# Two early transfers, the early weight conversions and one batch's halves, each issued sooner in a fused attention and mixer kernel

## The chip, the cores and the metric

The kernel runs on one core of one Trainium2 chip. The metric is device time in microseconds (us), from the first to the last instruction of the program with what the runtime adds around it, median of three runs.

## What is computed

Three layers follow each other; the arrays are float64, four batches, twelve heads, sequence 448, head size 64, so 768 features.

```python
# 1 attention with a sigmoid
scores = q @ k.T / 8 - log(448)
attn = (1 / (1 + exp(-scores))) @ v          # -> x [4, 448, 768]
# 2 mixer
h = x.T @ U @ V                              # along the sequence, U 448x32, V 32x448
u = x + h.T
x = u + relu(u @ w_ch1) @ w_ch2              # 768 -> 3072 -> 768
# 3 second mixer
theta = x @ w_theta
y = w_tok_r @ (x * cos(theta)) + w_tok_i @ (x * sin(theta))
u = x + y
out = u + relu(u @ w_ch)
```

## The kernel before

**Numbers in two halves.** Every matrix operand is split into a rounded high half and the rest (names ending in `h` and `l`), and a product is the sum of high by high, high by low and low by high. ScalarE makes the high half (`hi_act`, line 109), VectorE (`lo_dve`, line 121) or GpSimd (`lo_pool`, line 112) the low half by a subtraction.

**Attention.** Two heads form a pair; there are 24 pairs (`NP`), six to a batch, and the loop `for p in range(NP)` takes one after the other. For pair p it computes the scores in two parts, `QK(p, 0)` and `QK(p, 1)`, of two tiles `sc` each (line 386; 12 products a part). PSUM has two `sc` buffers, and ScalarE's sigmoid (line 390, tile `A`) frees them. `AV` (line 399) multiplies the `A` of pair p-1 by its values `v`, two of four steps after each part of the scores, into the one PSUM buffer `av`, which ScalarE empties into `X`. `XN(p-2)` (line 412) transposes a finished pair. While pair p is computed, VectorE prepares pair p+1: transposes into `kT` and `qT` (lines 364, 350), the high half `qh` (354) and the low halves `ql` and `kl` (121).

**The first mixer inside attention.** When a batch b is complete, `U1` (line 423, in pair 6b+8) and `U2` (line 448, tile `h`, in pairs 6b+9 to 6b+11) compute x.T @ U @ V for it and add it to `X`. `U2` needs `vcat`, the converted V.

**Conversions.** Weights come as float64 words. A `Conv` job turns one block into float32 halves in five steps: `size` (ScalarE, line 146; it also issues the load of the job after next), `shift` (VectorE, 150 and 153), `sign` (159, 162), `low` (167) and `fin`, which splits on ScalarE and GpSimd (183 and 184 for a weight, 112 and 115 for V). The nine early jobs are, in order, w1_0_0, U, V0, V1, w2_0_0, w1_0_1, w2_0_1, w1_1_0 and w2_1_0: 45 steps, handed out by `early_step()` one at a time. Before, two are handed out in each pair from pair 2 on, one between `K_hi(p + 1)` and `K_lo(p + 1)` and one at the pair's end, and what is left comes after the loop. Step 15 of 45, the `fin` of V0, so falls into pair 9 just ahead of `U2`.

**Queues.** The order on each engine is the order in which the program is written. Transfers are issued by SyncE's queue (SP) and a few at the start by ScalarE's. A pair takes four transfers of k, four of q (32x14x32) and two of v (112x4x64). Each transfer takes one of eight completion semaphores in turn (named DMAHW0 to DMAHW7 in the order below), and waits at its issue until the earlier transfer with the same semaphore has landed. Loads of k and q are issued four pairs ahead, of v three.

**The handover.** After the last pair, `split_u(0, ...)` makes the halves `uh` and `ul` of batch 0 (six columns d), the last pair's `AV` follows, then `split_u(1, ...)`, whose low halves go to GpSimd and VectorE in turn, `XN(22)`, and `ch1(0, 0)` (lines 620 to 622, tile `g`): two tiles of 18 products, which need the six `uh` and `ul` one after another.

Of the kernel before, what the change touches and what calls it, by code (L numbers as in the profile page):

```python
# [12 lines left out]
F32R = mybir.dt.float32r  # L13
# [11 lines left out]
def tile_kernel(  # L25
# [15 lines left out]
    nc = tc.nc  # L41
    B, H, S, D = q.shape
# [3 lines left out]
    P = 128  # L46
    CP = 112
    NC = S // CP
    NK = DM // P
# [40 lines left out]
    X = cpool.tile([P, NK, NT], F32, name="X")  # L90
# [9 lines left out]
    def pool(name, side="left", space=None):  # L100
        st = ExitStack()
        kw = dict(name=name, bufs=1, side=side, reuse_waits="tile")
        if space is not None:
            kw["space"] = space
        return st.enter_context(tc.tile_pool(**kw)), st


    def hi_act(o, i):
        nc.scalar.activation(o, i, AF.Copy)  # L109
# [10 lines left out]
    def lo_dve(o, i, h):  # L120
        nc.vector.tensor_sub(o, i, f(h))  # L121
# [187 lines left out]
    ap2, ap2_st = pool("ap2")  # L309
# [10 lines left out]
    def load_squares(eng, t, src):  # L320

        for h in range(2):
            for n in range(2):
                a = 2 * h + n
                eng.dma_start(
                    out=t[a * SQ:(a + 1) * SQ],
                    in_=src[h, :, n * SQ:(n + 1) * SQ].rearrange("(k i) j -> i k j", i=SQ),
                )

    def load_qk(p):  # L330
        b, hp = divmod(p, NH)
        h0 = 2 * hp
        kt = ap2.tile([P, NS, SQ], F32, tag="k", name=f"k_{p}", bufs=4)
        qt = ap2.tile([P, NS, SQ], F32, tag="q", name=f"q_{p}", bufs=4)
        load_squares(nc.sync, kt, k[b, h0:h0 + 2])
        load_squares(nc.scalar if p == 0 else nc.sync, qt, q[b, h0:h0 + 2])
        q_t[p], k_t[p] = qt, kt

    def load_v(p, eng=nc.sync):
        b, hp = divmod(p, NH)  # L340
        vt = ap1.tile([CP, 2, NC, D], F32, tag="v", name=f"v_{p}", bufs=4)
        for h in range(2):
            eng.dma_start(out=vt[:, h], in_=v[b, 2 * hp + h].rearrange("(c p) d -> p c d", p=CP))
        v_t[p] = vt

    def TQ(p):
        t = q_t.pop(p).rearrange("p k j -> p (k j)")
        x = ap2.tile([P, S], F32, tag="qT", name=f"qT_{p}", bufs=2)
        for n, s, m in runs(p // NH, 0, S):
            nc.vector.transpose(out=x[:, n:n + m], in_=t[:, s:s + m])  # L350
        h_ = ap2.tile([P, S], F32R, tag="qh", name=f"qh_{p}", bufs=2)
        l_ = ap2.tile([P, S], F32R, tag="ql", name=f"ql_{p}", bufs=2)
        if p:
            nc.vector.tensor_copy(h_, x)
        else:
            hi_act(h_, x)
        qq_t[p] = (h_, l_)
        return lambda: lo_dve(l_, x, h_)
# [3 lines left out]
    def TK(p):  # L362
        x = ap2.tile([P, S], F32, tag="kT", name=f"kT_{p}", bufs=2)
        nc.vector.transpose(out=x, in_=k_t.pop(p).rearrange("p k j -> p (k j)"))
        kT_t[p] = x

    def K_hi(p):
        h_ = ap2.tile([P, S], F32R, tag="kh", name=f"kh_{p}", bufs=2)
        l_ = ap2.tile([P, S], F32R, tag="kl", name=f"kl_{p}", bufs=2)
        kk_t[p] = (h_, l_)  # L370
        hi_act(h_, kT_t[p])

    def K_lo(p):
        h_, l_ = kk_t[p]
        lo_dve(l_, kT_t.pop(p), h_)

    def QK(p, half):


        (kh, kl), (qh, ql) = kk_t[p], qq_t[p]  # L380
        for c in (2 * half, 2 * half + 1):
            ps = ps_b.tile([P, 2, 512], F32, tag="sc", name=f"sc_{p}_{c}", bufs=2)
            for n, (a, b) in enumerate(((kh, qh), (kh, ql), (kl, qh))):
                for h in range(2):
                    sl = slice(h * D, (h + 1) * D)
                    nc.tensor.matmul(  # L386
                        ps[:CP, h, :S], a[sl, c * CP:(c + 1) * CP], b[sl], start=n == 0, stop=n == 2
                    )
            a = ap1.tile([CP, 2, S], F32, tag="A", name=f"A_{p}_{c}", bufs=6)
            nc.scalar.activation(a, ps[:CP, :, :S], AF.Sigmoid, bias=bias_s[:CP], scale=SCALE)  # L390
            A_t[p, c] = a

    def AV(p, c):
        b, hp = divmod(p, NH)
        if c == 0:
            av_t[p] = ps_a.tile([P, 512], F32, tag="av", name=f"av_{p}")
        ps = av_t[p]
        for h in range(2):
            nc.tensor.matmul(  # L399
                ps[h * D:(h + 1) * D, :S], v_t[p][:, h, c, :], A_t[p, c][:, h, :],  # L400
                start=c == 0, stop=c == NC - 1,
            )
        if c == NC - 1:
            hi_act(X[:, hp, b * S:(b + 1) * S], ps[:, :S])

    def XN(p):
        b, hp = divmod(p, NH)
        if hp == 0:
            xn_t[b] = ap.tile([CP, NC, DM], F32, tag="xn", name=f"xn_{b}")
        ps = ps_a.tile([P, 512], F32, tag="qx", name=f"xt_{p}")  # L410
        for c in range(NC):
            nc.tensor.transpose(ps[:CP, c * P:(c + 1) * P], X[:, hp, b * S + c * CP:b * S + (c + 1) * CP], ident)
        nc.vector.tensor_copy(
            xn_t[b][:, :, hp * P:(hp + 1) * P], ps[:CP].rearrange("p (c n) -> p c n", c=NC)
        )
# [20 lines left out]
    def u1_lo():  # L436

        while u1_t:
            ps, o = u1_t.pop()
            for g in range(3):  # L440
                x = ps[g * R:(g + 1) * R, :2 * P]
                sl = slice(2 * g * P, 2 * (g + 1) * P)
                for m in range(2):
                    lo_dve(o[(2 + m) * R:(3 + m) * R, sl], x, o[:R, sl])

    def U2(b, d, ps, vc, n=1):
        for m in range(n):
            nc.tensor.matmul(
                ps[:, m, :S], pc_t[b][:, (d + m) * P:(d + m + 1) * P], vc, start=True, stop=True
            )  # L450
        x = X[:, d:d + n, b * S:(b + 1) * S]
        nc.vector.tensor_add(x, ps[:, :n, :S], x)
# [75 lines left out]
    load_qk(0)  # L528
    nc.scalar.activation(warm, bias_s, AF.Sigmoid)
    load_v(0, nc.scalar)  # L530
    load_qk(1)
    load_qk(2)
    seq[0].load()
# [5 lines left out]
    def early_step():  # L539
        if esteps:  # L540
            esteps.pop(0).step()


    def warm_up(n):
        ps = ps_b.tile([P, 2, 512], F32, tag="sc", name=f"warm_{n}", bufs=2)
        for m in range(n):
            nc.tensor.transpose(ps[:, m % 2, :P], ident, ident)

    warm_up(36)
    TK(0)  # L550
    K_hi(0)
    lo_q = TQ(0)
    K_lo(0)
    lo_q()
    load_v(1, nc.scalar)
    for p in range(NP):
        nx = p + 1 < NP
        QK(p, 0)
        if nx:
            TK(p + 1)  # L560
            TQ(p + 1)()
        if p:
            AV(p - 1, 0)
            AV(p - 1, 1)
        if nx:
            K_hi(p + 1)
        if p > 1:
            early_step()
        if nx:
            K_lo(p + 1)  # L570
        b, r = divmod(p - 3 - NH, NH)
        if b >= 0 and r < NK // 2:
            U2(b, 2 * r, ps_a.tile([P, 2, 512], F32, tag="ux", name=f"h_{b}_{r}"), vcat[:, b % 2, :], 2)
        QK(p, 1)
        if p > 1:
            XN(p - 2)
        b, r = divmod(p - 2 - NH, NH)
        if b >= 0 and r == 0:
            U1(b, ap)
        if p:  # L580
            AV(p - 1, 2)
            AV(p - 1, 3)
        u1_lo()
        if p + 4 < NP:
            load_qk(p + 4)
        if 2 < p + 3 < NP:
            load_v(p + 3)
        if p == 0:
            seq[1].load()
        if p > 1:  # L590
            early_step()
    while esteps:
        early_step()
    ap2_st.close()
    ps_b_st.close()


    u01, u01_st = pool("u01", "right")
    ps_g, ps_g_st = pool("ps_g", "right", PSUM)
    uh_t, ul_t, g_t = {}, {}, {}  # L600

    def split_u(b, p, d0, d1, *los):
        if d0 == 0:
            uh_t[b] = p.tile([P, NK, S], F32R, name=f"uh{b}")
            ul_t[b] = p.tile([P, NK, S], F32R, name=f"ul{b}")
        for d in range(d0, d1):
            x = X[:, d, b * S:(b + 1) * S]
            hi_act(uh_t[b][:, d], x)
            los[d % len(los)](ul_t[b][:, d], x, uh_t[b][:, d])

    def ch1(i, b, js=range(FB)):
        if js[0] == 0:
# [34 lines left out]
            after(e2)  # L647


    split_u(0, u01, 0, NK, lo_dve)  # L650
    for c in range(NC):
        AV(NP - 1, c)
    ap1_st.close()
    uv, uv_st = pool("uv", "right")
    vlast = uv.tile([P, S], F32R, name="vlast")
    split_u(1, u01, 0, NK, lo_pool, lo_dve)
    XN(NP - 2)
    ch1(0, 0)
# [291 lines left out]
```

## Time and profile before

| | us |
|---|---|
| median of 3 runs | 1213.49 (1213.0 to 1218.13) |
| profiled execution, whole time | 1212.33 |
| its span, first to last instruction | 1210.5 |
| TensorE (PE) busy | 1178.9 (97%) |
| VectorE (DVE) busy | 784.4 (65%) |
| ScalarE (ACT) busy | 377.9 (31%) |
| GpSimd (POOL) busy | 298.9 (25%) |

The attention stage covers about the first 205 us of the span, the two big products of the first mixer the next 800, the second mixer the rest. PE is busy nearly everywhere; the 32 us in which it is not are spread over few places. A row of the timeline gives start, duration, engine, source line, operation, tile written from tiles read, and in brackets how long the engine had been idle and what released it. "x8" means eight instructions merged into one row. PEld is PE's weight load, SPq and ACTq are the issues of transfers.

### The profile page before, as it was taken

How to read it: one execution, taken by the hardware profiler on the slowest of the kernel's cores; microseconds unless marked ns; L12 is line 12 of the kernel's file. 1: busy time of each engine (PE TensorE's matmuls, PEld its weight loads, DVE VectorE, ACT ScalarE, POOL GpSimd, SP SyncE). 2: the span in 40 equal slices, each digit the busy share in tenths (PEclk: the TensorE clock that was granted, in tenths of full speed). 3: DMA queues.
4: the chain of work that ended last, by engine and by line, in shares of the span. 5: the costliest groups of instructions: out<-in, count | busy, mean ns of one | idle time of the engine just before them, and what ended most of it. 6: DMA issues, size and time to landing. Idle time of an engine off the chain costs nothing.

```text
span 1210.5 us, 15584 instructions
## 1 busy us (share of the span) xinstructions
PE 1178.9 (97%) x6220; PEld 1017.9 (84%) x6220; DVE 784.4 (65%) x955; ACT 377.9 (31%) x498; POOL 298.9 (25%) x170
## 2 busy tenths in 40 slices
PE   5979998999999999999999999999999999999998
PEld 3434444899999999999999999999999999999997
DVE  3656778456886678677867787969465733733443
ACT  3756786222221212122212221322123531531110
POOL 0111124232232314132322233434201512320000
PEclk7999999999999999999999999999999999999999
DMA  7664761001223122222322232333452000030344
GB/s 138 128 130 96 148 132 53 2 27 53 94 68 109 53 94 76 101 73 74 109 68 79 71 117 98 111 105 105 144 198 106 1 1 1 1 157 1 47 66 71
DMA packets 190808, 99.88 MB, mean 83 GB/s; under 512 B 158736, under 2 KB 182672, under 8 KB 190608
## 3 DMA queue, kind: packets, MB, share of 16 engines
q1 hardware_dynamic: 164752, 95.45, 28.2%
q10 hardware_dynamic: 25984, 3.44, 2.0%
q8 instruction: 49, 0.80, 0.3%
q14 instruction: 23, 0.19, 0.1%
HBM read 80.71 MB, written 18.15 MB: 82 GB/s over the span
## 4 chain that ended last, share of the span: by engine, by line
PE 92%; DVE 2%; SPq 2%; DMA 1%; ACT 1%; issue 1%; POOL 0%; ACTq 0%; DVEq 0%; POOLq 0%
PE g L621 10%; PE g L622 10%; PE g L620 10%; PE y L642 9%; PE y L644 9%; PE y L643 9%; PE av L399 5%; PE sc L386 5%; PE y L831 3%; PE y L832 3%; PE y L833 3%; PE th L754 2%; PE th L758 2%; PE th L755 2%; PE wc L912 2%; PE wc L913 2%
## 5 line engine op out<-in xcount | busy, mean ns | idle before, releaser
L621 PE MATMUL g<-ul,w 128*128 128x448 f32 x576 | 211.0, 366 | 2.6 <-DVE ul L121 2.6
L642 PE MATMUL y<-gh,w 128*128 128x448 f32 x576 | 211.3, 367 | 0.7 <-DVE X L646 0.7
L620 PE MATMUL g<-uh,w 128*128 128x448 f32 x576 | 210.8, 366 | 0.0
L644 PE MATMUL y<-gh,w 128*128 128x448 f32 x576 | 210.5, 365 | 0.0
L622 PE MATMUL g<-uh,w 128*128 128x448 f32 x576 | 210.5, 365 | 0.0
L643 PE MATMUL y<-gl,w 128*128 128x448 f32 x576 | 210.4, 365 | 0.0
L646 DVE TENSOR_TENSOR X<-y,X 128x896 f32<-128x896 f32 x144 | 156.3, 1087 | 79.1 <-PE y L644 77.6
L183 POOL TENSOR_TENSOR ca_w<-ca_w,w 128x768 f32<-128x768 f32 x48 | 90.3, 1881 | 470.0 <-ACT w L109 470.0
L627 ACT ACTIVATE gh<-g 128x896 fp32r<-128x896 f32 x48 | 44.1, 919 | 335.1 <-PE g L622 335.1
L621 PEld LDWEIGHTS g<-ul,w 128*128 128x128 f32 x576 | 108.2, 188 | 12.7 <-DVE ul L121 4.1
L628 DVE SCALAR_TENSOR_TENSOR gl<-g,gh 128x896 fp32r<-128x896 f32 x48 | 52.3, 1091 | 101.6 <-ACT gh L627 101.6
L642 PEld LDWEIGHTS y<-gh,w 128*128 128x128 f32 x576 | 108.2, 188 | 9.8 <-issue 1.1
L620 PEld LDWEIGHTS g<-uh,w 128*128 128x128 f32 x576 | 108.2, 188 | 9.1 <-issue 0.4
L644 PEld LDWEIGHTS y<-gh,w 128*128 128x128 f32 x576 | 108.2, 188 | 8.7
L622 PEld LDWEIGHTS g<-uh,w 128*128 128x128 f32 x576 | 108.2, 188 | 8.6
L643 PEld LDWEIGHTS y<-gl,w 128*128 128x128 f32 x576 | 108.2, 188 | 8.5
L390 ACT ACTIVATE A<-sc,bias_s 112x896 f32<-112x896 f32 x96 | 91.6, 1004 | 36.6 <-PE sc L386 24.3
L184 POOL TENSOR_TENSOR w<-ca_w,ws_w 128x768 fp32r<-128x768 f32 x48 | 96.1, 2003 | 3.8
L399 PE MATMUL av<-A,v 112*64 112x448 f32 x384 | 83.4, 557 | 0.6 <-ACT X L109 0.6
L112 POOL TENSOR_TENSOR zl<-t,zh 128x768 fp32r<-128x768 f32 x23 | 42.7, 1881 | 114.2 <-ACT zh L109 114.2
L146 ACT ACTIVATE ca_w<-ws_w 128x768 f32<-128x768 f32 x48 | 43.5, 906 | 61.0 <-POOL w L184 55.8
L831 PE MATMUL y<-tok,zh 128*128 128x448 f32 x168 | 61.7, 367 | 0.0
(145 smaller groups left out, 1867.8 us busy)
## 6 DMA issues: line engine op xcount, KB each, us to landing
ws_w<-in_moe_w_ch_dram SPq DMA_DIRECT2D x48, 768.0 KB, 4.5
k<-in_k_dram SPq DMA_DIRECT2D x96, 56.0 KB, 2.7
q<-in_q_dram SPq DMA_DIRECT2D x92, 56.0 KB, 2.4
v<-in_v_dram SPq DMA_DIRECT2D x44, 112.0 KB, 2.8
ws_th<-in_moe_w_theta_dram SPq DMA_DIRECT2D x6, 768.0 KB, 4.5
th_d<-sp_th SPq DMA_DIRECT2D x6, 768.0 KB, 6.3
ws_wc<-in_moe_w_ch_dram SPq DMA_DIRECT2D x6, 768.0 KB, 4.6
wc_d<-sp_wc SPq DMA_DIRECT2D x6, 768.0 KB, 7.0
```

The costliest lines, as they stand in the source:

```text
L183: eng.tensor_sub(a, a, f(o[:, 0]))
L184: eng.tensor_add(o[:, 1], a, e)
L390: nc.scalar.activation(a, ps[:CP, :, :S], AF.Sigmoid, bias=bias_s[:CP], scale=SCALE)
L399: nc.tensor.matmul(ps[h * D:(h + 1) * D, :S], v_t[p][:, h, c, :], A_t[p, c][:, h, :], start=c == 0, stop=c == NC - 1,)
L620: nc.tensor.matmul(o, wh[:, sl], uh_t[b][:, kk, :], start=kk == 0, stop=False)
L621: nc.tensor.matmul(o, wh[:, sl], ul_t[b][:, kk, :], start=False, stop=False)
L622: nc.tensor.matmul(o, wl[:, sl], uh_t[b][:, kk, :], start=False, stop=kk == NK - 1)
L642: nc.tensor.matmul(o, wh[:, sl], gh[:, j, :], start=j == 0, stop=False)
L643: nc.tensor.matmul(o, wh[:, sl], gl[:, j, :], start=False, stop=False)
L644: nc.tensor.matmul(o, wl[:, sl], gh[:, j, :], start=False, stop=j == FB - 1)
L646: nc.vector.tensor_add(x, ps[:, :, :S], x)
L831: nc.tensor.matmul(o, zh[:, sl], tok_h[:, i, :], start=n == 0, stop=False)
```

## The change

Three edits, and a function that moves with the third.

1. `load_v(1, nc.scalar)`, the values of pair 1, is written ahead of `load_qk(1)` instead of after the first pair's conversions.
2. `early_step()` is handed out from pair 1 on instead of pair 2, and a third time in pairs 4 and 6. Step 15, the `fin` of V0, falls into pair 7, and the last of the 45 into pair 22; none is left after the loop.
3. In the last pair the first three columns of `split_u(0, ...)` are written between `QK(23, 1)` and `XN(21)`, the other three at the loop's end. The memory of `ap2` (k, q and their halves) is given back there for it. `split_u` itself is unchanged and only stands earlier.

```diff
     load_qk(0)
     nc.scalar.activation(warm, bias_s, AF.Sigmoid)
     load_v(0, nc.scalar)
+    load_v(1, nc.scalar)
     load_qk(1)
     load_qk(2)
     seq[0].load()
...
     K_lo(0)
     lo_q()
-    load_v(1, nc.scalar)
     for p in range(NP):
...
             K_hi(p + 1)
-        if p > 1:
+        if p:
             early_step()
         if nx:
             K_lo(p + 1)
...
         QK(p, 1)
+        if not nx:
+            ap2_st.close()
+            u01, u01_st = pool("u01", "right")
+            split_u(0, u01, 0, 3, lo_dve)
         if p > 1:
             XN(p - 2)
...
         u1_lo()
+        if p in (4, 6):
+            early_step()
         if p + 4 < NP:
             load_qk(p + 4)
         if 2 < p + 3 < NP:
             load_v(p + 3)
         if p == 0:
             seq[1].load()
-        if p > 1:
+        if p:
             early_step()
+    split_u(0, u01, 3, NK, lo_dve)
     while esteps:
         early_step()
-    ap2_st.close()
     ps_b_st.close()
...
-    u01, u01_st = pool("u01", "right")
     ps_g, ps_g_st = pool("ps_g", "right", PSUM)
...
-    split_u(0, u01, 0, NK, lo_dve)
     for c in range(NC):
         AV(NP - 1, c)
```

ScalarE's order at the start and in pair 1 (`v_198` before and `v_114` now are the values of pair 1; `A_0` to `A_3` the sigmoids of a pair's four score tiles; `ca_w_0_0` the first step of job w1_0_0):

```order
 L343 DMA v_111<-in_v_dram 112x4x64 [waits DMAHW3_49]
-L109 ACTIVATE kh_188<-kT_186 128x448 [waits DVE_49]
-L109 ACTIVATE qh_193<-qT_191 128x448 [waits DVE_49]
-L343 DMA v_198<-in_v_dram 112x4x64 [waits DMAHW4_49]
-L343 DMA v_198<-in_v_dram 112x4x64 [waits DMAHW6_49]
+L343 DMA v_114<-in_v_dram 112x4x64 [waits DMAHW5_49]
+L343 DMA v_114<-in_v_dram 112x4x64 [waits DMAHW6_49]
+L109 ACTIVATE kh_191<-kT_189 128x448 [waits DVE_49]
+L109 ACTIVATE qh_196<-qT_194 128x448 [waits DVE_49]
 L390 ACTIVATE A_0_208<-sc_0_201,bias_s 112x896 [waits PE_49]
 L390 ACTIVATE A_1_217<-sc_1_210,bias_s 112x896 [waits PE_49]
...
 L109 ACTIVATE kh_303<-kT_290 128x448 [waits DVE_49,Activation_49]
...
+L146 ACTIVATE ca_w_0_0_311<-ws_w_0_0_137 128x768 [waits DMAHW4_49]
+L390 ACTIVATE A_2_321<-sc_2_314,bias_s 112x896 [waits PE_49,Activation_49]
```

The two issues move ahead of the first pair's high halves, and their semaphores were last used by transfers of pair 0 instead of pair 3; in pair 1 the first step of w1_0_0 now stands between two sigmoids.

SP's order after U's nine transfers, before (`k_330`, `q_331`, `v_340`: k and q of pair 5, values of pair 4; `ws_V_377`: V0):

```order
L278 DMA ws_U<-in_moe_U_dram 112x64 [waits DMAHW1_49]
L325 DMA k_330<-in_k_dram 32x14x32 [waits DMAHW2_49,DVE_49]
...
L325 DMA q_331<-in_q_dram 32x14x32 [waits DMAHW6_49,DVE_49]
...
L343 DMA v_340<-in_v_dram 112x4x64 [waits DMAHW2_49,PE_49]
L343 DMA v_340<-in_v_dram 112x4x64 [waits DMAHW3_49]
L289 DMA ws_V_377<-in_moe_V_dram 32x896 [waits DMAHW4_49]
```

and now (`ws_V_306`: V0; `k_337`, `q_338`: pair 5):

```order
L278 DMA ws_U<-in_moe_U_dram 112x64 [waits DMAHW1_49]
L289 DMA ws_V_306<-in_moe_V_dram 32x896 [waits DMAHW2_49]
L289 DMA ws_V_306<-in_moe_V_dram 32x896 [waits DMAHW3_49]
L289 DMA ws_V_306<-in_moe_V_dram 32x896 [waits DMAHW4_49]
L289 DMA ws_V_306<-in_moe_V_dram 32x896 [waits DMAHW5_49]
L325 DMA k_337<-in_k_dram 32x14x32 [waits DMAHW6_49,DVE_49]
```

V0's four transfers moved from behind pair 5's k and q to ahead of them.

VectorE's order around the last step of V0 ahead of its `fin`, before (`pc_924`: the result of `U1` for batch 0, pair 8; `kT_974`: pair 10):

```order
L121 TENSOR_TENSOR pc_924<-p_0_911,pc_924 32x256 x5
L167 SCALAR_TENSOR_TENSOR ws_V_377<-ws_V_377 128x448 [waits DVE_49]
L364 STREAM_TRANSPOSE kT_974<-k_750 128x448 [waits DMAHW2_49,DMAHW3_49,DMAHW1_49,DMAHW0_49]
```

and now (`kT_791`: pair 8):

```order
L159 SCALAR_TENSOR_TENSOR ca_V_688<-ws_V_306,ca_V_688 128x448 [waits DVE_49]
L162 TENSOR_SCALAR ws_V_306<-ca_V_688 128x448 [waits DVE_49]
L167 SCALAR_TENSOR_TENSOR ws_V_306<-ws_V_306 128x448 [waits DVE_49]
L364 STREAM_TRANSPOSE kT_791<-k_593 128x448 [waits DMAHW6_49,DMAHW7_49,DMAHW5_49,DMAHW4_49]
```

V0 is ready for its `fin` two pairs sooner, and no longer behind batch 0's `pc`.

## Rows read from the trace of the kernel before

**Rows 1.** Waits of PE over the span: total us, times, longest us.

```profile
PE sc L386 <- ACT A L390: 11.0, 1, 11.0
PE h L448 <- POOL vcat L115: 8.1, 1, 8.1
PE g L621 <- DVE ul L121: 2.6, 4, 0.7
```

**Rows 2.** Timeline of the first 34 us, ScalarE and PE.

```profile
4.39 0.86 ACTq L343 DMA_DIRECT2D v<-in_v_dram  x2
...
18.32 1.14 ACTq L343 DMA_DIRECT2D v<-in_v_dram  x2
...
19.51 1.91 ACT L390 ACTIVATE A<-sc,bias_s 112x896 f32<-112x896 f32 x2 [11.91 <-DMA k<-in_k_dram]
...
20.57 0.72 PE L386 MATMUL sc<-qh,kh 64*112 64x448 f32 x2 [10.97 <-ACT A L390]
...
25.24 1.73 PE L399 MATMUL av<-A,v 112*64 112x448 f32 x8
...
31.37 1.72 PE L399 MATMUL av<-A,v 112*64 112x448 f32 x8
...
33.19 0.90 ACT L146 ACTIVATE ca_w<-ws_w 128x768 f32<-128x768 f32 x1
```

**Rows 3.** Timeline: SP's issues of w1_0_0, of U, of pair 5's q, of V0.

```profile
12.41 0.48 SPq L201 DMA_DIRECT2D ws_w<-in_moe_w_ch_dram  x1
...
25.01 5.42 SPq L278 DMA_DIRECT2D ws_U<-in_moe_U_dram  x9
...
32.56 1.99 SPq L325 DMA_DIRECT2D q<-in_q_dram  x4
...
35.65 1.88 SPq L289 DMA_DIRECT2D ws_V<-in_moe_V_dram  x4
```

**Rows 4.** Issue to landing: first w1_0_0's one transfer, then pair 5's four of q.

```profile
DMA to landing us min/median/max: 5.1/5.1/5.1
...
DMA to landing us min/median/max: 2.2/2.2/2.5
```

**Rows 5.** Timeline: pair 1's q on VectorE, and PE's AV in pair 5.

```profile
10.21 0.65 DVE L350 STREAM_TRANSPOSE qT<-q 128x448 f32<-128x448 f32 x1 [0.64 <-DMA q<-in_q_dram]
...
11.32 0.62 DVE L121 TENSOR_TENSOR ql<-qT,qh 128x448 fp32r<-128x448 f32 x1
...
51.49 1.73 PE L399 MATMUL av<-A,v 112*64 112x448 f32 x8
```

**Rows 6.** Timeline: first scores of pairs 9, 10, 21 and 22 on PE.

```profile
78.77 0.46 PE L386 MATMUL sc<-qh,kh 64*112 64x448 f32 x2
...
97.09 0.46 PE L386 MATMUL sc<-qh,kh 64*112 64x448 f32 x2
...
178.07 0.46 PE L386 MATMUL sc<-qh,kh 64*112 64x448 f32 x2
...
185.76 0.46 PE L386 MATMUL sc<-qh,kh 64*112 64x448 f32 x2
```

**Rows 7.** Busy us (and instructions) of PE, PEld, DVE, ACT, POOL; PEclk; DMA share; GB/s.

```profile
90.00:97.00 7.00, 7.00 (x26) 3.57 (x26) 3.36 (x7) 2.01 (x2) 0.00 (x0) 0.54 0.01 2
```

**Rows 8.** Handover, 201 to 217 us: timeline, and all ul (ns min/median/max).

```profile
202.23 2.90 ACT L109 ACTIVATE uh<-X 128x448 fp32r<-128x448 f32 x6
202.41 1.84 POOL L183 TENSOR_TENSOR ca_w<-ca_w,w 128x768 f32<-128x768 f32 x1 [11.37 <-ACT w L109]
...
205.21 0.45 PE L620 MATMUL g<-uh,w 128*128 128x448 f32 x1
...
212.59 0.37 PE L620 MATMUL g<-uh,w 128*128 128x448 f32 x1
...
216.25 0.60 PE L412 MATMUL xt<-ident,X 128*112 128x128 f32 x4
...
L121 DVE TENSOR_TENSOR ul<-X,uh x9: 609/1564/2283, 202.8 to 212.9; 128x448 fp32r<-128x448 f32 x9
```

More of the change, by code (lines that the diff above doesn't have):

```diff
@@ L547, in warm_up, with split_u @@
             nc.tensor.transpose(ps[:, m % 2, :P], ident, ident)
+    uh_t, ul_t, g_t = {}, {}, {}
+    def split_u(b, p, d0, d1, *los):
+        if d0 == 0:
+            uh_t[b] = p.tile([P, NK, S], F32R, name=f"uh{b}")
+            ul_t[b] = p.tile([P, NK, S], F32R, name=f"ul{b}")
+        for d in range(d0, d1):
+            x = X[:, d, b * S:(b + 1) * S]
+            hi_act(uh_t[b][:, d], x)
+            los[d % len(los)](ul_t[b][:, d], x, uh_t[b][:, d])
     warm_up(36)
@@ L589, in tile_kernel @@
             seq[1].load()
-        if p > 1:
+        if p:
             early_step()
+    split_u(0, u01, 3, NK, lo_dve)
     while esteps:
         early_step()
-    ap2_st.close()
     ps_b_st.close()
-    u01, u01_st = pool("u01", "right")
     ps_g, ps_g_st = pool("ps_g", "right", PSUM)
[L600 to L609, printed above, removed]
     def ch1(i, b, js=range(FB)):
```

## The prediction

> **What bounds the kernel now.** I read first who PE waits for: three waits hold most of its idle time, 11.0 us at the scores, 8.1 at `h`, 2.6 at `g` [rows 1]. All three lie in attention and at its end, and each has one of the three edits beside it. Elsewhere PE works back to back, so a place is worth what its stall holds, and only until the next late thing.
>
> *The start.* ScalarE stands still for 11.91 us before the first sigmoids, put down to a transfer of k [rows 2]. In its queue the issues of pair 1's values stand just ahead, at 18.32 us: they waited for semaphores that pair 3's k held. PE's scores stop for want of a buffer (9.60 to 20.57), and the first `AV` comes at 25.24 [rows 2].
>
> *Pair 9.* `U2` waits for `vcat`, which GpSimd finishes only then. From pair 9's first scores to pair 10's it takes 97.09 - 78.77 = 18.32 us; the same work in pair 21, with no such wait, takes 185.76 - 178.07 = 7.69 [rows 6]. Behind the wait PE also runs at a mean granted clock of 0.54, so mostly at the lower level, 1.2 GHz, after 8.1 us without work [rows 1, 7].
>
> *The handover.* The first tile of `ch1(0, 0)` takes 212.59 - 205.21 = 7.38 us, the second, of the same 18 products, 216.25 - 212.59 = 3.66. The difference, 3.72, is waiting for `ul`, of which one takes 0.61 us at best, 1.56 in the median and 2.28 at worst while GpSimd works on the left-over conversion step and then on its own low halves [rows 8].
>
> **The change, part by part.**
>
> *Values of pair 1 sooner.* Their second issue now needs a semaphore of pair 0's q, landed by the time the first `qT` runs; the two issues cost 0.86 us on ScalarE at 4.39 for pair 0 [rows 2] and the next thing there waits for `kT` anyway, so I take 0.2, between 0 and 0.9. Score tile 0 is then turned by the sigmoid as soon as it is done, some 0.6 before 9.60, so at about 9.0. Before, `AV` followed the first sigmoid after 25.24 - 19.51 = 5.73 us [rows 2], part of it at the lower clock; I take 5.3 (4.8 to 5.7), which puts `AV` at 14.3 plus or minus 0.5, or **10.9 sooner**. That is the most the edit can give. Two things come late next.
>
> *Step 1 of w1_0_0 in pair 1.* It now stands ahead of two sigmoids and waits for its weights. SP issues those at 12.41 and they land 5.1 later [rows 3, 4]. SP's queue itself slips a little, because pair 1's q and pair 2's k now wait for semaphores of the two value loads; I take 0.5 (0 to 1.0, the length of a pair of value issues). So they land at 18.0, the step takes 0.90 [rows 2], and the sigmoids behind it start at 18.9 instead of about 17. The second `AV`, before at 31.37 and wanted at 20.5, comes at about 21.4: 18.9, two sigmoids (1.91 [rows 2]) and the eviction of `av`, for which I take the length of one `uh`, 0.5 [rows 8]. That is 1.0 lost, **9.9 left**.
>
> *Pair 5's q.* SP issues without a pause in this stretch, and what it does does not come sooner because PE does. U's nine transfers still end at 30.4, now 30.9 with the slip. V0's four (1.88) stand ahead of pair 5 [rows 3]. Pair 5's q was issued from 32.56 to 34.55, so now at 32.56 + 0.5 + 2.0 = 35.05 to 37.05; its last transfer is issued at about 36.6 and lands 2.4 later at 39.0 [rows 3, 4]. From a landing to the end of `ql` pair 1 shows 11.32 + 0.62 - 10.21 = 1.73 [rows 5]; then comes U's `shift`, which has a third of a weight's columns (0.6), and `kl` (0.62): 41.95. The `kl` products begin a third into the part, so `AV` follows 0.9 later at 42.85. Before it was at 51.49 [rows 5]: **8.65 sooner**, and that takes the place of the 9.9. The bounds: 9.9 if q comes in time, 7.0 if SP slips by 1.0 and issues a little slower still.
>
> *After pair 5* a pair takes (51.49 - 31.37) / 3 = 6.71 us on PE [rows 2, 5] and 5.1 on SP (1.99 each for k and q, 1 for v), so SP gains 1.6 a pair, less what V1 (eight issues, 3.8) and w2_0_0 take. Adding these up, q of pair 8 and of pair 10 arrive between 0.1 and 1 us ahead of need. I charge nothing, at worst 2.
>
> *V0 two pairs sooner.* Its `fin` moves from pair 9 to pair 7; GpSimd's four operations need some 5 us there and have two pairs, 13.4. `U2` then waits for `pc` alone, as in pair 21. So 18.32 becomes 7.69 plus 0.3 for the `kl` of the next pair, which VectorE's fuller queue delays: **10.3 sooner** (9 to 10.6). It contains the 8.1 of waiting and 2.5 to 2.9 of the lower clock. Every issue it moves (V1, w2_0_0) was counted above on SP.
>
> *Halves of batch 0.* Three `uh` (3 x 0.48 = 1.45) now stand on ScalarE ahead of the eviction that the last `AV` waits for. ScalarE was idle for 0.9 just there, so the last `AV` starts 0.56 later. Against that, no conversion step is left for GpSimd at 202.41, three `ul` are done before and three take 0.62 each under the last `AV` (3.2 us of PE). The 3.72 of waiting goes: **3.1 sooner** (2.0 to 3.7). The cover is those 3.2 us; if GpSimd still slowed the three, 1 to 2 us would come back.
>
> **Sum.** 8.65 + 10.3 + 3.1 = 22.05. The profiled execution of 1212.33 would take 1190.3; it lies 1.16 below the median of the runs shown, so 1213.49 - 22.0 = 1191.5.
>
> **Two rules of the Trainium skill.** "DMA: Bandwidth & Descriptors", section "Issuing engines are not separate DMA queues", says that transfers started by several engines interleave on the same 16 DMA engines, and that issuing them elsewhere saves only sequencer time, usually little. By that the values put ahead would delay pair 1's q by their own transfer and the first term would shrink by up to 1 us. The rows above differ in what is short: the issue, 0.5 us each, sets SP's pace. "TensorE: Matmul & The Clock Gate", section "A second HAM failure mode: psum-queue depth-cycling", says that pauses between groups of matmuls that wait for PSUM buffers can bring the clock down again. By that the first pairs, which are paced by two score buffers, would run at 1.2 GHz; it is rival 2 below.
>
> **Rivals.**
>
> 1. *The wait moves to SP.* Pairs 5, 8 and 10 all wait for q, because one of the long issues falls badly. For it: the margins of 0.1 to 1 us. Against: SP gains 1.6 a pair. Price: 2 to 4 us; time 1193.5 to 1195.5.
> 2. *The clock falls in the first two pairs.* Between 9 and 14 us PE works in bursts, each waiting for a sigmoid. Rows at the lower clock show 7 us of work where 4.2 do [rows 7], so up to 2.9 lost, of which 1.2 lie under the wait for pair 5's q. Against: before, the clock fell only behind 8 and 11 us without work. Time about 1193.
> 3. *`U2` finds something else late.* `pc`, `kl` or pair 10's q take the place of `vcat`, and half of the 10.3 stays. Pair 21 speaks against it. Time 1196 to 1198.
> 4. *It does not do what it says at the start.* ScalarE still stands before the sigmoids, because the value loads' semaphores come late. Against: the order shows them free with pair 0's q. The first term would go: about 1200.
> 5. *Slower than before.* Every transfer waits for the one eight before it. Ten transfers a pair then take 10/8 of a landing time: at 2.4 us that is 3.0 and hidden, at the 5.1 of w1_0_0 6.4 and just hidden under 6.71. From 5.4 on it decides. With v brought forward, conversions and k and q crowding each other until landings average 6.5 over pairs 2 to 21, each pair loses 1.4, 28 us in all against 22 gained: 1220. Against: SP's rate of issue, and with it the traffic, does not rise, since SP was already issuing without pause.
>
> **How the numbers follow.** Forecast 62%, rival 1 16%, rival 2 8%, rival 3 7%, rival 4 5%, rival 5 2%. The bounds of the terms, 7.0 to 9.9, 9 to 10.6 and 2.0 to 3.7, give 18 to 24.2, so 1189.3 to 1195.5; the runs of one kernel differ by some 2 us more. From 1187 to 1198 holds the forecast, rivals 1 and 2 and most of 3. A measurement can tell about 0.5%, 6 us. Faster by more than that is everything but rival 5 and a double failure: 0.95, same 0.03, slower 0.02.
>
> **What would show it.** In the trace of the changed kernel: the first sigmoid at about 9 us and `AV` at 14.3; one wait of about 1 us for line 146 in pair 1; VectorE waiting for pair 5's q until about 39 and `AV` at 42.9; no wait of `h` on `vcat` and no low clock after the first pairs; `ch1(0, 0)`'s two tiles of equal length, 3.7 us. The forecast is wrong if PE has a wait of over 3 us anywhere before 200 us, or if the last `AV` starts over 1 us after its predecessor's eviction could.

## The result, and the profile after

| | before | after |
|---|---|---|
| median, us | 1213.24 (1212.8 to 1218.13, 4 runs) | 1195.67 (1195.33 to 1195.86, 4 runs) |
| ratio, 95% interval | | 0.9846 (0.9821 to 0.9871) |
| span of the profiled execution | 1210.5 | 1193.6 |
| PE busy in it | 1178.9 | 1177.1 |

The change took 17.6 us off the median and 16.9 off the span; the forecast was 22.0 and 1191.5, its range 1187 to 1198. PE's busy time fell by 1.8 us only, so nearly all of what went is waiting.

The waits of PE in the changed kernel (total us, times, longest us) answer [rows 1]:

```profile
PE sc L386 <- DVE kl L121: 2.1, 3, 1.0
PE sc L386 <- DVE qh L354: 1.4, 2, 1.1
...
PE h L448 <- DVE pc L121: 1.2, 3, 0.4
PE sc L386 <- DVE ql L121: 1.1, 2, 0.9
```

All three old waits, of 11.0, 8.1 and 2.6 us, are gone. In their place stand short ones behind `kl`, `qh` and `ql`, which VectorE makes: the next late thing is a pair's own k and q.

To see where the lead arises and where it goes, one instruction that both kernels have is looked up at each place. `AV(p)` is the product with the `A` of pair p, and runs in pair p+1.

| place on PE | before | after | lead | forecast |
|---|---|---|---|---|
| first `AV(0)` | 25.24 [rows 2] | 14.93 | 10.3 | 10.9 |
| first `AV(1)` | 31.37 [rows 2] | 21.59 | 9.8 | 9.9 |
| first `AV(4)` | 51.49 [rows 5] | 43.34 | 8.15 | 8.65 |
| first `AV(7)` | 71.61 | 67.27 | 4.3 | 8.65 |
| pair 9's first scores | 78.77 [rows 6] | 75.38 | 3.4 | 8.65 |
| pair 10's first scores | 97.09 [rows 6] | 83.14 | 13.95 | 18.95 |
| pair 22's first scores | 185.76 [rows 6] | 171.80 | 13.96 | 18.95 |
| `xt` behind `ch1(0, 0)`'s first two tiles | 216.25 [rows 8] | 199.39 | 16.86 | 22.05 |

Of the 5.2 us that are missing at the end, 0.5 were missing at `AV(4)` and 4.8 go between `AV(4)` and pair 9. Everything else came within 0.3.

The start of the changed kernel, from the timeline of ScalarE and PE (start, us, engine, line, operation, tile written from tiles read, and in brackets the idle time before and what ended it), against [rows 2]:

```profile
4.43 1.95 ACTq L343 DMA_DIRECT2D v<-in_v_dram  x4
...
8.95 1.91 ACT L390 ACTIVATE A<-sc,bias_s 112x896 f32<-112x896 f32 x2 [1.42 <-PE sc L386]
...
14.93 1.72 PE L399 MATMUL av<-A,v 112*64 112x448 f32 x8
...
18.01 0.93 ACT L146 ACTIVATE ca_w<-ws_w 128x768 f32<-128x768 f32 x1 [1.20 <-DMA ws_w<-in_moe_w_ch_dram]
...
21.59 1.72 PE L399 MATMUL av<-A,v 112*64 112x448 f32 x8
```

The four value issues stand together, the first sigmoids follow the scores at 8.95, and line 146 waits for w1_0_0 until 18.01 (forecast 18.0).

Pair 1's q pays for it. SP issues its four transfers from 6.13 us before and from 6.29 now, but behind pair 1's values they take longer from issue to landing, before and now:

```profile
DMA to landing us min/median/max: 2.4/2.7/3.1
...
DMA to landing us min/median/max: 3.7/4.0/4.1
```

SP, VectorE and PE up to pair 5, in the timeline of the changed kernel, against [rows 3] and [rows 5]:

```profile
26.33 4.54 SPq L278 DMA_DIRECT2D ws_U<-in_moe_U_dram  x9
30.92 1.82 SPq L289 DMA_DIRECT2D ws_V<-in_moe_V_dram  x4
...
34.86 1.99 SPq L325 DMA_DIRECT2D q<-in_q_dram  x4
...
39.48 0.65 DVE L350 STREAM_TRANSPOSE qT<-q 128x448 f32<-128x448 f32 x1 [2.13 <-DMA q<-in_q_dram]
```

U ends at 30.87 and pair 5's q is issued at 34.86, with V0's four ahead of it; VectorE waits for that q until 39.48. It then takes the path of the forecast (`ql`, U's `shift`, `kl`), and `AV(4)` starts at 43.34.

Now the place that was not in the sum. This is pair 8's q on SP, and VectorE, GpSimd and PE around it:

```profile
50.40 3.68 SPq L289 DMA_DIRECT2D ws_V<-in_moe_V_dram  x8
54.18 1.94 SPq L325 DMA_DIRECT2D k<-in_k_dram  x4
56.22 3.12 SPq L325 DMA_DIRECT2D q<-in_q_dram  x4
...
59.87 1.13 POOL L112 TENSOR_TENSOR ca_V<-ca_V,vcat 32x448 f32<-32x448 f32 x1 [15.05 <-ACT vcat L109]
...
61.47 0.70 DVE L350 STREAM_TRANSPOSE qT<-q 128x64 f32<-128x64 f32 x2 [2.81 <-DMA q<-in_q_dram]
...
62.64 1.44 DVE L121 TENSOR_TENSOR ql<-qT,qh 128x448 fp32r<-128x448 f32 x1
62.75 0.45 PE L386 MATMUL sc<-qh,kh 64*112 64x448 f32 x2 [0.62 <-ACT X L109]
63.68 1.41 POOL L115 TENSOR_TENSOR vcat<-ca_V,ws_V 32x448 fp32r<-32x448 f32 x1
64.01 1.57 DVE L121 TENSOR_TENSOR kl<-kT,kh 128x448 fp32r<-128x448 f32 x1
64.14 0.46 PE L386 MATMUL sc<-ql,kh 64*112 64x448 f32 x2 [0.93 <-DVE ql L121]
...
65.63 0.58 PE L386 MATMUL sc<-qh,kl 64*112 64x448 f32 x2 [1.03 <-DVE kl L121]
```

Two things meet here. V1's eight transfers stand ahead of pair 8's k and q on SP, and q's four issues take 3.12 us instead of 1.99, so VectorE stands 2.81 us for q. One of the four, 1.61 us long, makes all of the excess (the view of tile q on SP at 57.3 us: duration in ns, start):

```profile
L325 SPq DMA_DIRECT2D q<-in_q_dram x1: 1610/1610/1610, 57.2 to 57.2; - x1
```

The four GpSimd steps of V0's `fin` run from 59.87 to 65.09, just while VectorE then makes `ql` and `kl`. Those two subtractions, 0.62 us each elsewhere [rows 5], take 1.44 and 1.57. PE waits three times in 3.5 us, 0.62, 0.93 and 1.03; the first of these products reads `qh`, which is ready at 62.61, though the profile names `X`, which ended 0.1 later. Behind that its clock falls, as the windows show (length; busy us and instructions of PE, PEld, DVE, ACT, POOL; granted clock; DMA share; GB/s):

```profile
60.00:65.60 5.60, 3.04 (x16) 1.09 (x15) 4.06 (x6) 2.58 (x4) 4.88 (x4) 1.00 0.73 129
65.60:69.80 4.20, 4.17 (x16) 1.70 (x16) 4.00 (x9) 2.48 (x3) 0.00 (x0) 0.59 0.90 245
69.80:76.00 6.20, 6.20 (x56) 3.36 (x56) 0.77 (x2) 4.00 (x8) 0.00 (x0) 1.00 0.84 146
```

At a mean of 0.59, mostly the level of 1.2 GHz, 4.2 us hold what 2.5 would: 1.7 lost. With the 2.6 of waiting that makes 4.3 of the 4.8 us.

`U2` and the handover, in the timeline of the changed kernel, against [rows 6] and [rows 8]:

```profile
75.38 0.46 PE L386 MATMUL sc<-qh,kh 64*112 64x448 f32 x2
...
78.92 0.65 PE L448 MATMUL h<-vcat,pc 128*128 128x448 f32 x2 [0.41 <-DVE pc L121]
...
83.14 0.46 PE L386 MATMUL sc<-qh,kh 64*112 64x448 f32 x2
...
188.31 3.23 PE L399 MATMUL av<-A,v 112*64 112x448 f32 x16 [1.05 <-ACT X L109]
...
189.13 1.69 DVE L121 TENSOR_TENSOR ul<-X,uh 128x448 fp32r<-128x448 f32 x3
...
191.87 0.45 PE L626 MATMUL g<-uh,w 128*128 128x448 f32 x1
...
195.67 0.37 PE L626 MATMUL g<-uh,w 128*128 128x448 f32 x1
...
199.39 0.60 PE L412 MATMUL xt<-ident,X 128*112 128x128 f32 x4
```

From pair 9's to pair 10's first scores it takes 7.76 us, 18.32 before, and `U2` waits 0.41 for `pc`. The three `ul` under the last `AV` take 1.69 us together, and `ch1(0, 0)`'s two tiles 3.80 and 3.72 us, 7.38 and 3.66 before.

### The profile page after: what moved, and what is told of

Its sections match the earlier page's. It is cut to its first block, busy times and chain, and to the rows that moved or that the text cites. A ratio compares the mean times of both kernels' runs of the same rounds, so it can differ in the third digit from the quotient of the medians.

```text
span 1193.6 us, 15586 instructions
## 1 busy us (share of the span) xinstructions
PE 1177.1 (99%) x6220; PEld 1016.0 (85%) x6220; DVE 783.5 (66%) x955; ACT 377.4 (32%) x498; POOL 298.1 (25%) x170
## 4 chain that ended last, share of the span: by engine, by line
PE 90%; DVE 3%; SPq 3%; DMA 2%; ACT 1%; issue 1%; ACTq 0%; DVEq 0%
PE g L626 10%; PE g L627 10%; PE g L628 10%; PE y L648 10%; PE y L650 10%; PE y L649 10%; PE av L399 3%; PE y L837 3%; PE y L838 3%; PE y L836 3%; PE sc L386 3%; PE th L759 2%; PE th L763 2%; PE th L760 2%; PE wc L919 2%; PE wc L917 2%
```

## The experiments

Three sets; the kernels of a set ran on one chip beside the kernel before (median 1213.68, 1215.26 and 1214.84 us). "Handover" is measured from the third step of `AV(22)` to the first product behind `ch1(0, 0)`'s two tiles and the transpose: 17.32 us before, 14.21 after. The changed kernel was not run again beside them; where a kernel is compared with it, the places in the two profiles are.

### Set 1: which edit gives what

**Edit 1 alone** (against the kernel before).

```diff
     load_v(0, nc.scalar)
+    load_v(1, nc.scalar)
     load_qk(1)
...
     lo_q()
-    load_v(1, nc.scalar)
```

> The kernel before with the first edit alone (pair 1's values issued ahead of pair 1's k and q). If the three edits act at separate places: AV of pair 0 at about 15 us as in the changed kernel, the 8.1 us wait of U2 for V0 and the 3.7 us of waiting at the handover stay; 10 us less than before, 1203. If the start's gain is given back at the next late transfer: AV of pair 4 later than 43 us and 1206 or more.

Measured: 1205.17 us (1202.76 to 1208.86), ratio 0.9925 (0.9898 to 0.9952). `AV(0)` starts at 15.38, `AV(1)` at 23.13, `AV(4)` at 43.26. The waits of PE keep the two other entries, and the windows show a lower clock in the first pairs:

```profile
PE h L448 <- POOL vcat L115: 8.1, 1, 8.1
PE g L621 <- DVE ul L121: 2.5, 4, 0.7
...
15.00:20.00 5.00, 5.00 (x26) 1.97 (x22) 2.29 (x4) 2.61 (x4) 0.00 (x0) 0.66 1.11 230
```

Edit 1 touches its own place alone: 8.2 us of lead at `AV(4)` and 8.0 still at `U2` (81.94 against 89.97). It did so although rival 2 occurred: the clock was 0.66 between 15 and 20 us, behind scores that had waited 1.4 us for a sigmoid, and `AV(1)` came 1.5 later than in the changed kernel. From there `AV(4)` follows after 20.13 us, three pairs of 6.71 without a wait; the changed kernel is level with it at `AV(4)` because it loses about as much there to pair 5's q. So `AV(4)` came later than the 43 us of the second expectation, but for the clock and not for a late transfer, and the 1203 us were missed by 2. The waits after pair 5 don't appear here: the conversions, and with them V1's loads and V0's `fin`, are still two pairs later.

**Edit 2 alone** (against the kernel before).

```diff
-        if p > 1:
+        if p:
             early_step()
...
+        if p in (4, 6):
+            early_step()
...
-        if p > 1:
+        if p:
             early_step()
```

> The kernel before with the second edit alone (early steps from pair 1 on, a third one in pairs 4 and 6). U2 no longer waits for V0: 10.3 us less. If GpSimd's left-over step is what stretches the handover, that goes too, since no step is left after the loop: another 3.4, so 1199.5. If the earlier halves of the third edit are needed for the handover: 1203.

Measured: 1199.08 us (1198.62 to 1199.26), ratio 0.9872 (0.9853 to 0.9891). The wait of 11.0 us at the start stays, that on `vcat` is gone, and the handover takes 13.81 us, 3.5 less than before, with `split_u` where it was. Its six `ul`, on the timeline of VectorE, run at full speed:

```profile
192.59 3.30 DVE L121 TENSOR_TENSOR ul<-X,uh 128x448 fp32r<-128x448 f32 x6 [2.02 <-ACT uh L109]
```

So taking the left-over conversion step off GpSimd is by itself enough for the handover; the halves need not move.

**Edit 3 alone** (against the kernel before: `split_u` in two parts as in the change, steps and values as before).

```diff
         QK(p, 1)
+        if not nx:
+            ap2_st.close()
+            u01, u01_st = pool("u01", "right")
+            split_u(0, u01, 0, 3, lo_dve)
...
+    split_u(0, u01, 3, NK, lo_dve)
     while esteps:
```

> The kernel before with the third edit alone (three of batch 0's halves inside the last pair). The left-over conversion step stays on GpSimd ahead of the other three low halves. If it is what stretches them: 1.5 to 2.5 us less than before, 1211. If the earlier halves carry the handover: 3.1 less, 1210.

Measured: 1209.12 us (1208.54 to 1209.52), ratio 0.9956 (0.9939 to 0.9973). The handover takes 14.07 us, 3.25 less than before, with the left-over step still there. VectorE and GpSimd show why:

```profile
203.30 1.69 DVE L121 TENSOR_TENSOR ul<-X,uh 128x448 fp32r<-128x448 f32 x3
203.76 2.94 POOL L183 TENSOR_TENSOR ca_w<-ca_w,w 128x768 f32<-128x768 f32 x1 [13.16 <-ACT w L109]
```

The two overlap, and here it is GpSimd that is drawn out (2.94 us, against 1.84 [rows 8]), while each `ul` keeps its 0.62. That either edit removes the wait, and both together no more than one, was not in the forecast, which set the 3.1 beside edit 3 and counted on the left-over step being gone as well.

**Edits 1 and 2** (the changed kernel without edit 3).

```diff
-        if not nx:
-            ap2_st.close()
-            u01, u01_st = pool("u01", "right")
-            split_u(0, u01, 0, 3, lo_dve)
...
-    split_u(0, u01, 3, NK, lo_dve)
...
+    split_u(0, u01, 0, NK, lo_dve)
     for c in range(NC):
```

> The changed kernel without the third edit (first and second alone). If the handover's gain comes from GpSimd having no step left: the last AV starts 0.4 us sooner and the low halves keep up under it, so 0.4 less than the changed kernel, 1195.3. If the earlier halves carry it: 3 us more, 1198.7.

Measured: 1194.75 us (1192.43 to 1196.87), ratio 0.9835 (0.9813 to 0.9858). The handover takes 13.80 us, 0.4 less than with edit 3, whose three `uh` stand on ScalarE ahead of an eviction that the last `AV` waits for (1.05 us there in the changed kernel). Up to pair 8 the code is that of the changed kernel, but in this execution pair 5's q came later, because the last of its four issues, at 36.77, took 1.83 us; VectorE's timeline and a window:

```profile
41.33 0.65 DVE L350 STREAM_TRANSPOSE qT<-q 128x448 f32<-128x448 f32 x1 [3.60 <-DMA q<-in_q_dram]
...
42.00:48.00 6.00, 4.99 (x18) 2.29 (x20) 5.54 (x14) 2.48 (x3) 0.74 (x1) 0.58 0.65 116
```

`AV(4)` starts at 45.95, 2.6 later than in the changed kernel, and behind the waits the clock falls just as it did there in pair 8. `AV(7)` then starts at 67.87, 0.6 later than there: nothing is lost in pair 8, whose q is there in time and whose `kl` is made before GpSimd begins. So in these two executions what SP couldn't deliver in time was paid once, at one place or the other. The gains of the edits do not add up: at `xt` (216.25 before) edit 1 alone is 8.6 ahead, edit 2 alone 13.0, and both together 17.6 instead of 21.6.

### Set 2: the two suspects of pair 8

Theory: pair 8's q is late because V1 stands ahead of it on SP, and its low halves are slow because GpSimd works on V0 beside them; the loss needs both. Rivals: q's lateness alone makes it, or GpSimd alone. All four kernels are the changed kernel with one thing moved.

**V0's `fin` later**: pair 7's middle step is left out, so `fin` falls to the end of the pair.

```diff
-        if p:
+        if p and p != 7:
             early_step()
```

> The changed kernel with the middle early step of pair 7 left out, so that V0's last step, with its four operations on GpSimd, comes at the end of pair 7 instead of ahead of kl of pair 8; all later steps come half a pair later. If GpSimd stretches ql and kl of pair 8 (1.44 and 1.57 us in the changed kernel): these take 0.62 each, AV of pair 7 comes 1.8 to 2.5 us sooner, the clock does not fall, 2.5 to 3.5 less than the changed kernel, 1192.5. If the lateness of q alone sets pair 8: no more than 0.5 less.

Measured: 1191.36 us (1191.06 to 1192.96), ratio 0.9805 (0.9789 to 0.982). VectorE and GpSimd in pair 8:

```profile
60.87 0.70 DVE L350 STREAM_TRANSPOSE qT<-q 128x64 f32<-128x64 f32 x2 [3.06 <-DMA q<-in_q_dram]
...
62.04 0.63 DVE L121 TENSOR_TENSOR ql<-qT,qh 128x448 fp32r<-128x448 f32 x1
...
62.58 0.62 DVE L121 TENSOR_TENSOR kl<-kT,kh 128x448 fp32r<-128x448 f32 x1
...
64.06 1.13 POOL L112 TENSOR_TENSOR ca_V<-ca_V,vcat 32x448 f32<-32x448 f32 x1 [18.49 <-DMA q<-in_q_dram]
```

With GpSimd still idle the two subtractions take 0.63 and 0.62 us, PE waits for nothing in pair 8, the clock is 1.00 from 60 to 70 us, and `AV(7)` starts at 64.25, 3.0 sooner. But more than `fin` differs. q comes 0.6 sooner, its four issues taking 1.99 us here, and PE comes 0.7 later, because its clock was low in the first pairs (a window):

```profile
15.00:20.00 5.00, 5.00 (x26) 1.95 (x26) 2.97 (x6) 3.74 (x5) 0.00 (x0) 0.73 1.07 226
```

Seen from PE, q is 1.3 us less late than in the changed kernel, so this run does not show what a late q alone would cost. An estimate from the changed kernel's rows: at 0.62 each, 0.54 apart as here, `ql` and `kl` would have been ready at 63.26 and 63.80 there and, with the clock kept up, `AV(7)` would have started at about 64.9. That leaves some 1.4 of the 4.8 us to q alone.

**V1 later**: V1 is loaded behind pair 8's k and q and pair 7's values.

```diff
+        if p == 4:
+            plan["V1"].load()
```

(and it is taken out of the chain in which each job loads the one after next)

> The changed kernel with V1's eight transfers issued behind k, q of pair 8 and the values of pair 7 instead of ahead of them. If q of pair 8 comes late because SP is behind: it lands 3.7 us sooner, pair 8 waits for nothing and the clock does not fall, 4.8 less than the changed kernel, 1191. If GpSimd alone sets it: kl of pair 8 is still stretched, 1194 to 1196.

Measured: 1191.66 us (1191.06 to 1192.04), ratio 0.9804 (0.9789 to 0.9818). VectorE and GpSimd in pair 8:

```profile
57.24 0.66 DVE L350 STREAM_TRANSPOSE qT<-q 128x64 f32<-128x64 f32 x2
...
59.36 0.62 DVE L121 TENSOR_TENSOR kl<-kT,kh 128x448 fp32r<-128x448 f32 x1 [0.37 <-ACT kh L109]
59.93 1.14 POOL L112 TENSOR_TENSOR ca_V<-ca_V,vcat 32x448 f32<-32x448 f32 x1 [14.42 <-ACT vcat L109]
```

VectorE doesn't wait for q at all, `kl` is finished just as GpSimd begins, and `AV(7)` starts at 64.12. So with V1 out of the way the loss is gone, and V1's place on SP is shown to be a cause of it. As q comes early, the two engines do not meet either, so this run does not part the two suspects.

**V0 later**: V0 is loaded, in the same way, behind pair 5's k and q and pair 4's values.

```diff
+        if p == 1:
+            plan["V0"].load()
```

> The changed kernel with V0's four transfers issued behind k, q of pair 5 and the values of pair 4, as they stood in the kernel before. q of pair 5 lands 1.9 us sooner, so AV of pair 4 keeps the lead of AV of pair 1 (9.8 us instead of 8.15). If q of pair 8 sets what is left of the lead, that is all given back there: 1195.7, no change. If not: 1194.

Measured: 1196.73 us (1195.9 to 1197.73), ratio 0.9849 (0.9831 to 0.9867). `AV(4)` starts at 41.83, 1.5 sooner than in the changed kernel, and `AV(7)` at 66.93, 0.3 sooner: what is won in pair 5 is given back in pair 8. The same things meet there again: q's issues take 3.08 us, `ql` and `kl` 1.46 and 1.55 beside GpSimd, PE waits 0.97, 0.94 and 0.91, and the clock is 0.50 from 64.0 to 70.6.

**Both later.**

```diff
+        if p == 1:
+            plan["V0"].load()
+        if p == 4:
+            plan["V1"].load()
```

> The changed kernel with both V0's transfers behind pair 5's and V1's behind pair 8's. If SP's lateness is what took the lead at both places: lead of 9.3 to 9.8 us kept to pair 8, 5.5 to 6.5 less than the changed kernel, 1189.7. If GpSimd sets pair 8: 1193 to 1195.

Measured: 1190.59 us (1190.02 to 1191.47), ratio 0.9796 (0.9781 to 0.9811). `AV(4)` starts at 42.31, `AV(7)` at 62.77, and the clock is 1.00 in every window up to 85 us. VectorE and GpSimd in pair 8:

```profile
58.59 1.14 POOL L112 TENSOR_TENSOR ca_V<-ca_V,vcat 32x448 f32<-32x448 f32 x1 [15.80 <-ACT vcat L109]
58.65 1.56 DVE L121 TENSOR_TENSOR kl<-kT,kh 128x448 fp32r<-128x448 f32 x1
```

Here `kl` is drawn out again (1.56 us), and it costs nothing, because q was there early. So the slow subtraction alone is hidden. A late q without it was not seen in any of these runs; what it costs rests on the estimate above.

### Set 3: a better version, and the order at the start

**Without edit 3, V0 and V1 later, one step in pair 1.**

```diff
-        if p:
+        if p > 1:
             early_step()
```

(the step between pair 1's sigmoids; `split_u` as in the kernel before; V0 and V1 as in the last)

> Built from the two delays: V0 is loaded behind pair 5's k and q, V1 behind pair 8's k, q and values, edit 3 is left out, and pair 1 hands out one conversion step instead of two, so that none stands between its sigmoids and V0's last step falls at the end of pair 7. If the cause at pair 8 is q's lateness together with GpSimd's V0, nothing waits there: 1190.6 of the two delays, less 0.4 for edit 3, less up to 1.0 for the step that no longer stands ahead of the second AV: 1189.2 to 1190.2. If the gain of the two delays came from another order of the steps instead, the step that moves brings the loss back: about 1194.

Measured: 1189.84 us (1189.76 to 1190.39), ratio 0.9794 (0.977 to 0.9818); span 1188.5, 1188.2 in the last kernel. The handover gives its 0.4 (13.81 us). The step's 1.0 us is won at `AV(1)`, 21.18 against 22.18, and is gone at `AV(4)`, 42.43 against 42.31: again pair 5's q sets that time. In pair 6 it then falls behind, to 63.74 at `AV(7)` against 62.77, so that its time meets the expectation while the gains behind it do not add up as expected. Of all kernels run this one has the lowest median, but from the last one it can't be told apart.

**The same, with pair 1's values behind its k and q, on SP.**

```diff
     load_v(0, nc.scalar)
-    load_v(1, nc.scalar)
     load_qk(1)
+    load_v(1)
     load_qk(2)
```

> As the last, with pair 1's values issued by SP behind pair 1's k and q instead of by ScalarE ahead of them. If a transfer put ahead only delays what is issued behind it, pair 1's k and q land 0.7 to 1.4 sooner and the first AV comes at about 14.2 instead of 14.9, while SP runs 1.0 later from pair 2 on; pair 5's q was in time by about that much, so within 1 us of the last. If the issuing engine matters more than the order, the values come late to the AV of pair 1 and that step starts over 2 us later than in the last.

Measured: 1190.84 us (1190.23 to 1191.94), ratio 0.98 (0.9776 to 0.9824). `AV(0)` starts at 13.99, 1.05 sooner than in the last kernel, and `AV(4)` at 41.54, 0.9 sooner. In pair 6 q is late, and PE's clock falls; PE's timeline and a window:

```profile
47.82 0.45 PE L386 MATMUL sc<-qh,kh 64*112 64x448 f32 x2 [0.90 <-DVE qh L354]
...
50.00:54.00 4.00, 4.00 (x19) 1.52 (x17) 2.49 (x6) 2.91 (x4) 0.00 (x0) 0.64 0.74 135
```

`AV(7)` comes at 65.24, 1.5 later than in the last kernel. So the values put ahead do delay pair 1's k and q, by about 1 us, and the later issue on SP takes it back.

## Why the prediction was right, and where not

**The start: right in kind, 0.1 us outside its bound.** Forecast 14.3 (plus or minus 0.5) for `AV(0)`, measured 14.93. The missing 0.6 is what the prediction priced at up to 1 us and left out of the sum: pair 1's q took 3.7 to 4.1 us to land instead of 2.4 to 3.1, and VectorE got pair 1's k at 9.61 instead of 8.93 and its q at 11.62 instead of 10.21 [rows 5]. The rule of the Trainium skill in "DMA: Bandwidth & Descriptors", section "Issuing engines are not separate DMA queues", says that transfers of several issuers share the same DMA engines; the trace agrees, by those 3.7 to 4.1 us, and `AV(0)` came 1.05 sooner in the last experiment, where the values stand behind. The same section of the Trainium skill also says that the time to start a transfer is usually small beside the transfer. One issue is so here too, 0.5 us against 2.2 to landing [rows 3, 4]; but the issues follow one another, the four of a pair's q take 1.99 us on SP [rows 3], and it is SP's pace that set `AV(4)`, `AV(5)` and `AV(7)` in one kernel or another.

**w1_0_0 in pair 1: right**, the step starts at 18.01 and `AV(1)` at 21.59 (18.0 and 21.4). It turned out to be worth nothing by itself, as pair 5's q takes its place.

**Pair 5's q: right**, 39.48 against 39.0, `AV(4)` 43.34 against 42.85. The excess is the 0.5 of q alone. But one execution is no bound: in the kernel without edit 3 the same q came at 41.33, behind one issue of 1.83 us, outside the 7.0 us that the prediction kept as its lower end (lead 5.5).

**After pair 5: the step that failed.** "q of pair 8 and of pair 10 arrive between 0.1 and 1 us ahead of need. I charge nothing, at worst 2." It measured 4.8. The sum of SP's times was nearly right (V1's issues took 3.68 us, 3.8 was put in); three things lay outside it. q's own four issues took 3.12 us instead of 1.99, one of them 1.61, which turned a margin of a few tenths into a wait of 0.6. `fin` of V0, which edit 2 moves from pair 9 to pair 7, was costed on GpSimd alone ("some 5 us there and have two pairs"), and not on VectorE, whose `ql` and `kl` it drew out from 1.24 to 3.01 us. And three waits of 0.6 to 1.0 us were followed by the lower clock, at a cost of 1.7. The prediction had the price of such a meeting in its own rows, 0.61 us against 1.56 to 2.28 for `ul` [rows 8], and used it for the handover only. The rule in the Trainium skill's "SBUF — State Buffer", section "Who interferes with whom", would have named it: a VectorE instruction with two inputs in SBUF contends with a GpSimd instruction that reads SBUF. `ql` and `kl` are of that kind; the trace agrees with 0.62 against 1.44 and 1.57. This was rival 1, "one of the long issues falls badly", right for pair 8 and not for pair 10, at 2 to 4 us; the slow subtraction and the clock were not in it. The slow subtraction alone cost nothing where q was early; a late q alone would have cost some 1.4 us by the estimate above. The 16.9 to 17.6 us that were gained lie below the 18 to which the lower bounds of the terms add up; the range held the result because it had been stretched for the rivals.

**`U2`: right**, 18.32 to 7.76, forecast 7.99.

**The handover: size right, cause half right.** Forecast 3.1, measured 2.9 to 3.1. The prediction set it beside the halves; edit 2 alone gives 3.5, and edit 3 on top takes 0.4 back by the three `uh` ahead of an eviction, for which the prediction had put 0.56.

**The rivals.** Rival 2 occurred in edit 1 alone, at 0.66 from 15 to 20 us, and with V0's `fin` or V1 later, at 0.73 and 0.75. It did not in the profile of the changed kernel, where the clock stayed at 1.00 until pair 8, nor in the four others that issue pair 1's values on ScalarE ahead of its k and q. The rule in the Trainium skill's "TensorE: Matmul & The Clock Gate", section "A second HAM failure mode: psum-queue depth-cycling", thus has three profiles here for it and five against. In the three, `AV(1)` came 1.0 to 1.5 us later than in the changed kernel; in all eight PE had waited in the first two pairs for buffers or for `qh`. Rivals 3, 4 and 5 did not occur. The prediction's test, a wait of over 3 us on PE, would have missed the fault: the longest wait in pair 8 was 1.03 us. Its sign "no low clock after the first pairs" shows it, at 0.59 from 65.6 to 69.8.

## What to carry to other kernels

When a step moves on one engine, look for what the engine beside it will run at that moment, and price the meeting by the slowest rows of the same operation. Where a queue of issues paces several consumers, a lead won ahead of one of them holds only until the next thing that this queue delivers late, so the order in the queue decides how much of an early start is kept: two loads put behind the ones that were needed gave about 5 us more. Where two edits remove the same wait, run each alone; one of them may only cost.

## What the hardware showed that was not expected

- **Short waits can be followed by the lower clock.** In pair 8 of the changed kernel PE's longest wait was 1.03 us; with two others, 0.62 and 0.93, inside 3.5 us it was followed by a mean of 0.59 for 4.2 us. With V0 later it was 0.50 from 64.0 to 70.6 us, beside and behind waits of 0.97, 0.94 and 0.91. Before, the clock was low only behind 8 and 11 us without work [rows 1, 7]. Waits of this size do not always do it: the first pairs kept the clock in five kernels and lost it in three.
- **Now and then one issue on SP takes three times as long as the others.** In all nine kernels with pair 1's values early, one issue that starts between 35.5 and 38.9 us takes 1.2 to 1.8 us, and in eight of them another between 56.3 and 59.3 takes 1.3 to 1.9; most issues around them take 0.3 to 0.5. What counts is the transfer that stands there. It was pair 5's q in the kernel with edits 1 and 2, where that q came latest, and pair 8's q in the changed kernel and with V0 later, the two kernels that lost lead in pair 8; in the others it was another transfer, and pair 8 lost nothing. Why such an issue takes long stays open.
- **VectorE and GpSimd slow each other, and which one pays differs.** GpSimd's V0 steps took 1.13 us alone and up to 1.41 beside `ql` and `kl`, which went from 0.62 to 1.44 and 1.57; in the kernel with edit 3 alone it was the reverse, GpSimd's step 2.94 us and `ul` untouched. What decides is not settled by these runs.
- **Products at two rates with the same clock shown.** In the profile of edit 1 alone, PE, busy throughout, completes fewer products in 60 us from about 720 us on, at a granted clock of 1.00 in both stretches (windows of that kernel):

```profile
640.00:700.00 60.00, 60.00 (x298) 55.59 (x297) 47.43 (x49) 13.19 (x16) 17.50 (x9) 1.00 0.22 74
760.00:820.00 60.00, 60.00 (x292) 54.50 (x291) 48.09 (x48) 13.59 (x16) 23.71 (x13) 1.00 0.31 106
```

  Up to the end of that stage 3.5 us of the lead (8.6 to 5.1) were lost by it, in one profile alone, and where nothing had been edited. The cause stays open; it is a reason to compare kernels by the lead at a place beside the time of the whole run.
